# First block of an attention and MoE chain: U kept in SBUF from float32 products on 64x32 tiles, attention by head parity, added sums by DMA, a written issue order

## The chip, the cores and the metric

The kernel runs on one core of one Trainium2 chip. The metric is the device time of one execution in microseconds. Before, three runs took 1742.01, 1742.24 and 1744.55 us.

## What is computed

Slot attention over 8 batches, 8 heads, 576 tokens of width 64 and 32 slots, then two MLP blocks (512 to 2048 to 512) over all 4608 tokens. Weights come as float64.

```python
a   = softmax(phi, over tokens)                 # per slot
k_m = einsum('bhsm,bhsd->bhmd', a, k); v_m = einsum('bhsm,bhsd->bhmd', a, v)
attn = softmax(q @ k_m^T / 8, over slots)
x   = attn @ v_m                                # [4608, 512], heads side by side
x   = relu(x @ w_in)**2 @ w_out                 # first block
h   = x @ w_in2
out = (h - tanh(h)) @ w_out2                    # second block
```

## The kernel before, in words

Every product that needs float32 accuracy is split into a rounded part and a rest (fp32r), and three products are summed.

- **Attention, first half** (`att_a`, lines 169 to 260), for four heads of one batch: the softmax of phi over tokens, then `vkm` (line 216, 96x32 tiles, float32) and its transpose, which gives k_m and v_m.
- **U = v_m @ w_in** (lines 262 to 331). x is never formed; the first block multiplies attn by U, 256 rows (head, slot) by 2048 columns per batch. Batches 0 and 1 get U head group by head group (`u_first`). Batches 2, 3 and 4 to 7 are two groups: w_in's split lies in DRAM (`w_d`), `u_pair` computes a head for all batches of the group (lines 311, 312), copies it out, stores it to DRAM (`u_d`, line 315), and `u_load` (line 330) reads one batch's 512 columns back. U is held as float32.
- **Attention, second half** (`att_b`, lines 336 to 398), for half a batch: transpose q, scores, softmax over slots, transposes on VectorE, split into `at`.
- **First block** (`l1_step`, lines 446 to 503): units of 288 tokens, 16 units, 16 hidden tiles each, so 256 steps. A step casts 128 columns of U (450), subtracts (452), makes six products h (459), relu (463), the square (467 on ScalarE for s < 72, 469 on VectorE after), the split gh, gl (473, 475), and twelve products with w_out into four PSUM banks (483 to 485). The first four units take the hidden tiles in two halves; the sum of the first half goes to DRAM (503), comes back (512) and is added on VectorE (492).
- **Weights** (`conv`, lines 123 to 145): float64 words are made into float32 by one ScalarE and four VectorE instructions (133 to 143); `split` makes the fp32r pair on ScalarE and POOL (148, 150). The second block's weights are split in the first block, stored as pairs (`w2_d`) and loaded from POOL near its end (545, 551).
- **Second block** (lines 557 to 654): 144 steps of 12 products with w_in2 (595), the polynomial for h - tanh h (607 to 615), the split (624, 625), 12 products with w_out2 (639 to 641). `x2_load` splits x2 (576, 579).
- **Order.** The start, up to about step 36 of the first block, follows the string `ORDER`, one stage per word. From there tables of step numbers (`ATT_A`, `ATT_B`, `U_ALL`, `U_LOAD`, `W2_CONV`) say at which step a generator begins; each tick lets every active generator go on by one stage, and the framework's scheduler sets the order on the engines. Each engine then works its list in order; a DMA is issued in order by SyncE or POOL.

Of the kernel before, what the change touches and what calls it, by code (L numbers as in the profile page):

```python
# [41 lines left out]
ORDER = """
i0 i0 i0 i0 i1 c4 i0 c1 i1 c4 c4 c2 k0 i0 c1 i1 c2 i1 c13 b0 i0 c4 i0 c1 b0 b0 c0 i0 c2 c3 c1 i0 i0 c2 b0 b2 i0 c0 k1 c4 b0 c9 i1 b2 i1 i0 b2 b0 c0 i0 b2 c2 i1 b0 i0 b0 b1 c3 b2 b2 c3 i1 c9 c9 i1 c0 b0 b3 b1 b1 i1 b2 c1 i1 b0 b1 c7 b2 c5 c3 b1 i1 c9 b0 b5 i1 c0 i1 c9 u00 b2 c5 b5 b5 u00 b2 i1 b1 b5 b1 c3 c5 b0 c6 c5 b0 c6 b2 b3 b5 c7 b1 b1 b5 b0 c6 u01 u01 b1 b0 k2 i2 b3 b1 b3 s1 b3 c8 t2 i2 b2 b3 b1 c12 c6 t1 b3 s2 b1 c26 i2 b1 b1 s1 i2 s2 b3 c10 t3 c5 s0 b4 c12 i2 c11 s1 s0 i2 s0 s1 c6 c8 s0 s2 i2 c8 s1 c10 s0 i2 i2 c10 c8 i2 c8 c13 t0 s1 s2 s0 s1 c10 s2 b2 s3 b3 c12 b2 u02 s0 i2 u02 c11 c14 c11 c12 c10 s0 s3 b3 b2 b4 i2 i2 b3 s2 c11 c11 i2 i2 c7 c14 b4 s1 u03 b3 u10 c26 b4 b4 b3 u03 c13 b3 s2 c7 b3 c25 s3 c12 s2 b4 s4 s6 s5 s5 c25 s3 c7 c15 s3 s5 s5 s3 s4 b4 s6 c14 s4 s5 c13 s6 s8 s8 s3 s7 t11 c13 s4 s5 s6 s6 s7 s5 s4 c15 i3 c25 s3 s8 s4 s6 s10 k3 s4 c15 s8 s5 s7 s9 s8 s9 s4 c14 s7 s11 s9 c15 c30 s6 c14 s6 s7 s7 u10 c15 s9 s8 s10 s9 c26 s9 s7 i3 s10 s7 c17 s11 i3 s8 i3 s10 s11 s13 c26 s8 s10 s7 s14 s10 s7 i3 c30 s9 s14 c26 b4 s14 c25 s12 b4 c17 b7 s7 i3 s9 s12 c25 s13 s12 b7 s11 c17 i3 s14 s11 i3 b7 s12 i3 b4 s13 s15 s12 s12 i3 i3 s10 s11 u12 b7 b4 i3 b4 i3 i3 s14 u12 s12 s13 s11 s13 i3 c16 s10 s14 b5 s15 u11 c16 b5 b6 b5 b7 c17 b5 s15 b6 u11 s17 s14 b4 s11 c22 s13 b5 b6 b5 s19 s12 s15 s13 s14 s17 s15 c17 s16 b4 c30 s15 b6 s16 b6 b5 b4 b5 t10 b7 t26 t8 c16 b5 b6 s18 s13 s16 s15 s16 c28 b6 s17 b6 c30 s15 u13 c30 s16 c16 b6 s16 s19 s15 c16 s17 b6 s18 c29 b7 s17 s18 t9 s15 s16 b6 s19 s16 b7 s17 c22 u13 s18 b6 c20 b6 c19 s20 s19 s20 s21 b6 s17 s23 s19 s20 s23 s21 c22 s18 c19 b7 s18 s17 b6 s15 s20 s20 s22 s20 s18 s22 b7 s21 s18 s20 s29 c22 b7 s22 s20 s19 s19 b7 s19 s22 s29 s21 c19 s24 c20 b7 s23 b7 u04 s21 s21 c28 t25 s21 s25 s23 s22 s21 c18 b7 c20 s24 s23 c22 c20 s23 t16 s22 s29 c28 s22 c20 t17 c29 s29 s24 s25 s22 s30 s29 s24 s26 c28 c24 s23 s25 s24 s24 s25 s23 s24 u04 s27 s23 c28 c29 c29 c19 s25 s28 u14 c29 s27 c19 s25 s26 s26 s23 s28 c18 s26 s27 s24 s29 c27 s26 c18 s26 s31 s23 c27 c18 s27 s25 s30 s31 c21 s26 s28 c24 s27 c18 s25 s26 s28 t18 u05 s27 u05 s28 s33 s29 s28 s27 s32 s31 c27 s33 s30 s31 s30 s32 c23 s34 c21 s30 s29 s28 s32 s30 c24 s31 s35 s28 c23 s31 s31 t19 c21 s35 c23 c21 s30 s33 c21 u14 s33 s34 c27 s33 c24 c31 s32 c23 s27 s32 u15 s33 s30 c24 s33 c31 c27 c31 s32 s31 s34 s34 u06 c23 u07 u15 u06 s32 s31 u07 s35 s36 s34 s36 s32 s34 s34 s35 c31 t27 s35 c31 t24 s31
"""
# [3 lines left out]
ATT_A = (29, 33, 36, 39, 61, 65, 68, 71, 82, 76, 79, 86)  # L48
ATT_B = (47, 60, 76, 95, 107, 124, 146, 156, 176, 193, 205, 220)
U_ALL = (45, 46, 47, 48, 52, 52, 53, 54, 40, 56, 53, 54, 59, 55, 61, 62, 96, 95, 107, 108, 99, 100, 105, 101,  # L50
    110, 103, 120, 109, 113, 116, 125, 127)
U_LOAD = (58, 63, 63, 70, 88, 88, 78, 101, 123, 127, 129, 134, 143, 143, 150, 163, 181, 177, 177, 192, 193,
    200, 207, 222)
W2_CONV = (72, 68, 68, 76, 76, 83, 88, 88, 114, 115, 116, 123, 117, 128, 131, 130, 137, 139, 141, 149, 148,
    151, 160, 152, 166, 160, 179, 174, 185, 212, 207, 178)
# [7 lines left out]
def moe_chain_kernel(ctx: ExitStack, tc: tile.TileContext, q, k, v, phi, w1i, w1o, w2i, w2o, out):  # L63
    nc = tc.nc
    w1i, w1o, w2i, w2o = (w.bitcast(I32) for w in (w1i, w1o, w2i, w2o))
    out_v = out.rearrange("(b p c) e -> b c p e", b=B, c=NC)
# [42 lines left out]
    km_t = [a_km.tile([P, 4, 64], F32, name=f"km{i}") for i in range(5)]  # L109
    # v_m: for batches 0, 1 heads 0 to 3 of a group in 6 blocks of M columns: v0, v1, 0, 0, v2, v3; then [head, batch, M].  # L110
    vm = [a_v.tile([P, 32, M], F32R, name=n) for n in ("vh", "vl")]
    vh, vl = (t.rearrange("p (h b) m -> p h (b m)", h=H) for t in vm)
    v_done, v_read, s_done = set(), set(), set()
    for t in vm:
        nc.gpsimd.memset(t.bitcast(F32), 0.0)
    for t in km_t:
        nc.gpsimd.memset(t, 0.0)

# [1 line left out]
    raws = [p_raw, p_wob, p_u, p_u] + [p_raw, p_wob] * 12  # L120
    n_raw = [0]

    def conv(src, out):
        raw = slot(raws[n_raw[0]] if n_raw[0] < len(raws) else p_raw, [P, 512, 2], "raw", I32)
        n_raw_of = n_raw[0]
        n_raw[0] += 1
# [5 lines left out]
        f = slot(p_t, [P, 512], "wf")  # L132
# [19 lines left out]
    def half(o):  # L152
        return slice(64 * o, 64 * o + 64)
# [15 lines left out]
    def att_a(b, g, p_kv, ps, fine):  # L169
# [13 lines left out]
        if fine:  # L183
            yield
# [6 lines left out]
        if fine:  # L191
            yield
# [31 lines left out]
        if fine:  # L224
            yield
# [529 lines left out]
```

## Time and profile before

| What | Value |
|---|---|
| median of three runs | 1742.24 us |
| span of the profiled execution | 1736.6 us |
| TensorE busy | 1622.8 us (93%) |
| VectorE busy | 1331.5 us (77%) |
| ScalarE busy | 837.0 us (48%) |
| POOL busy | 721.6 us (42%) |
| moved by DMA | 185.27 MB |
| mean granted TensorE clock | 0.971 |

The page gives the profiled execution's own time as its span, from the first to the last instruction, 5.6 us under the median. Busy times are unions of overlapping instructions of one engine; shares are averages over stages with different limits, so the rows below are read by stretch.

### The profile page before, as it was taken

What the parts mean: (1) busy time and instruction counts of PE and PEld (TensorE: products, weight loads), DVE (VectorE), ACT (ScalarE), POOL (GpSimd) and SP (SyncE); (2) the same over time, 40 slices, a digit from 0 to 9 for tenths busy, and PEclk for the clock granted to TensorE, in tenths of its full rate; (3) what the DMA queues carried; (4) which work ended last, traced back from release to release, by engine and by line L of the source; (5) the groups of instructions that cost most, each with busy time, mean ns of one, the idle gap of its engine ahead of it and who ended that gap; (6) DMA issues with size and microseconds to landing.
All of it is one profiled execution on the core that took longest, in us unless ns stands there. A gap on an engine that the chain in (4) does not pass through costs nothing.

```text
span 1736.6 us, 27125 instructions
## 1 busy us (share of the span) xinstructions
PE 1622.8 (93%) x9488; PEld 1392.4 (80%) x9488; DVE 1331.5 (77%) x2016; ACT 837.0 (48%) x1875; POOL 721.6 (42%) x721
## 2 busy tenths in 40 slices
PE   5799997689998889999999999999999999999998
PEld 3588885578876788999998888888888888888887
DVE  7989642269635778785754898989898989898987
ACT  4677653245533555555554444444444444444343
POOL 4566532146533445554475342424242423232222
PEclk9899998789999999999999999999999999999999
DMA  9655664367845655341367010101010000000000
GB/s 256 200 172 191 192 183 146 103 183 224 251 141 186 209 173 182 113 161 55 104 222 238 1 38 12 31 19 31 19 28 22 26 24 25 25 7 25 1 25 25
DMA packets 114248, 185.27 MB, mean 107 GB/s; under 512 B 14272, under 2 KB 74688, under 8 KB 114112
## 3 DMA queue, kind: packets, MB, share of 16 engines
q1 hardware_dynamic: 104896, 149.99, 28.2%
q0 software_dynamic: 9216, 33.56, 6.1%
q8 instruction: 74, 1.21, 0.3%
q14 instruction: 62, 0.51, 0.1%
HBM read 124.52 MB, written 58.98 MB: 106 GB/s over the span
## 4 chain that ended last, share of the span: by engine, by line
PE 71%; DMA 13%; DVE 9%; issue 3%; POOL 2%; ACT 1%; SPq 0%; DVEq 0%; POOLq 0%; ACTq 0%
PE h L595 22%; DMA u_d<-ust 9%; PE o L641 8%; PE o L639 8%; PE o L640 8%; PE h L459 7%; PE acc L484 5%; PE acc L483 5%; PE acc L485 5%; DVE usp L452 1%; DVE wf L138 1%; DVE wf L143 1%; DVE wf L135 1%; DMA xs<-x_d 1%; DVE wf L137 1%
## 5 line engine op out<-in xcount | busy, mean ns | idle before, releaser
L625 POOL TENSOR_TENSOR gl<-pl,gh 128x512 fp32r<-128x512 f32 x144 | 206.1, 1431 | 519.2 <-ACT gh L624 519.2
L595 PE MATMUL h<-x2h,wi 128*128 128x512 f32 x1152 | 379.8, 391 | 0.0
L475 POOL TENSOR_TENSOR gl<-gg,gh 128x288 fp32r<-128x288 f32 x256 | 227.6, 891 | 316.5 <-ACT gh L473 267.2
L483 PE MATMUL acc<-gh,wo 128*128 128x288 f32 x1024 | 311.8, 305 | 18.9 <-DVE xs L492 16.6
L484 PE MATMUL acc<-gl,wo 128*128 128x288 f32 x1024 | 311.8, 304 | 5.5 <-POOL gl L475 5.4
L485 PE MATMUL acc<-gh,wo 128*128 128x288 f32 x1024 | 309.4, 302 | 0.0
L459 PE MATMUL h<-aT,usp 128*128 128x288 f32 x1536 | 272.7, 311 | 22.5 <-ACT r L463 9.6
L459 PEld LDWEIGHTS h<-aT,usp 128*128 128x128 f32 x1536 | 224.5, 195 | 43.7 <-issue 13.4
L595 PEld LDWEIGHTS h<-x2h,wi 128*128 128x128 f32 x1152 | 216.2, 188 | 46.4
L607 ACT ACTIVATE u<-h 128x512 f32<-128x512 f32 x144 | 86.2, 599 | 332.2 <-PE h L595 327.3
L639 PE MATMUL o<-wo,gh 128*128 128x512 f32 x576 | 225.4, 391 | 0.9 <-ACT gh L624 0.9
L641 PE MATMUL o<-wo,gl 128*128 128x512 f32 x576 | 224.9, 391 | 0.7 <-POOL gl L625 0.7
L640 PE MATMUL o<-wo,gh 128*128 128x512 f32 x576 | 224.3, 389 | 0.0
L595 PE MATMUL h<-x2l,wi 128*128 128x512 f32 x576 | 224.1, 389 | 0.0
L483 PEld LDWEIGHTS acc<-gh,wo 128*128 128x128 f32 x1024 | 200.5, 196 | 20.5 <-DVE xs L492 17.5
L484 PEld LDWEIGHTS acc<-gl,wo 128*128 128x128 f32 x1024 | 201.1, 196 | 8.5 <-POOL gl L475 8.2
L469 DVE TENSOR_TENSOR gg<-r 128x288 f32<-128x288 f32 x184 | 121.4, 660 | 112.2 <-ACT r L463 56.4
L485 PEld LDWEIGHTS acc<-gh,wo 128*128 128x128 f32 x1024 | 200.4, 196 | 0.0
L611 DVE SCALAR_TENSOR_TENSOR pl<-pl,u 128x512 f32<-128x512 f32 x144 | 184.0, 1278 | 4.5
L473 ACT CAST gh<-gg 128x288 fp32r<-128x288 f32 x256 | 110.0, 431 | 155.5 <-DVE gg L469 83.2
L452 DVE TENSOR_TENSOR usp<-u,usp 128x256 fp32r<-128x256 f32 x256 | 142.8, 561 | 41.4 <-ACT usp L450 41.1
L610 DVE SCALAR_TENSOR_TENSOR pl<-u 128x512 f32<-128x512 f32 x144 | 117.9, 819 | 43.0 <-ACT u L607 40.2
(100 smaller groups left out, 2643.7 us busy)
## 6 DMA issues: line engine op xcount, KB each, us to landing
raw<-in_moe_w_out SPq DMA_DIRECT2D x32, 512.0 KB
raw<-in_moe_w_in SPq DMA_DIRECT2D x32, 512.0 KB
ws<-w_d POOLq DMA_DIRECT2D x32, 512.0 KB, 6.8
w_d<-ws SPq DMA_DIRECT2D x32, 512.0 KB
u<-u_d SPq DMA_DIRECT2D x24, 512.0 KB
x_d<-xs SPq DMA_DIRECT2D x80, 144.0 KB
kv<-in_v SPq DMA_DIRECT2D x64, 144.0 KB
kv<-in_k SPq DMA_DIRECT2D x64, 144.0 KB
```

What stands on the lines that cost most here:

```text
L452: nc.vector.tensor_tensor(us[:, 1], src, us[:, 0].bitcast(F32), op=ALU.subtract)
L459: nc.tensor.matmul(t[:, :HT], us[:, w, g, :], x, start=(n == 0), stop=(n == 5))
L475: nc.gpsimd.tensor_tensor(gl, gg, gh.bitcast(F32), op=ALU.subtract)
L483: nc.tensor.matmul(o, wh[:, c], gh, start=(f == a), stop=False)
L484: nc.tensor.matmul(o, wh[:, c], gl, start=False, stop=False)
L485: nc.tensor.matmul(o, wl[:, c], gh, start=False, stop=(f == z - 1))
L595: nc.tensor.matmul(t, wi[f][:, w, c, :], x, start=(n == 0), stop=(n == 11))
L611: stt(pl, pl, A1, u, op0=ALU.add, op1=ALU.mult)
L625: nc.gpsimd.tensor_tensor(lo, pl, hi.bitcast(F32), op=ALU.subtract)
L639: nc.tensor.matmul(o, gh[:, c], wh, start=(f == 0), stop=False)
L640: nc.tensor.matmul(o, gh[:, c], wl, start=False, stop=False)
L641: nc.tensor.matmul(o, gl[:, c], wh, start=False, stop=(f == FT - 1))
```

## The change

- **U.** w_in stays float32 (`w1`, no split). `u_make` multiplies v_m of one head (64x32, at rows 0 to 63 or 64 to 127 of the array by the head's parity and at 32 columns by its pair) by 512 columns, eight products into two banks (line 246), and writes cast and rest of 512 columns straight into an SBUF tile that the steps read (250, 251). Four such tiles exist, so a tile is made once both units of the batch before have read theirs. `u_d`, `w_d`, the stores and loads of U and the per-step cast are gone. w_in is kept in DRAM as float32 (135) and reloaded for each batch from 2 on, 1 MB for 512 columns (140).
- **Attention.** `att_b` takes four heads of one parity over the whole batch: scores as eight 64x32 products into two banks (293), softmax on 128x576. `att_a` adds tokens in two halves.
- **First block.** The square is always on ScalarE (386). The half sums of the first four units are added in DRAM by an accumulating DMA that POOL issues (417). `tmp` has six buffers, not eight.
- **Second block's weights** are stored as float32 (431) and split after the reload (438, 446 with `split`): w_out2 and seven tiles of w_in2 in the last 22 steps of the first block, nine tiles of w_in2 in the second block's first steps.
- **Order.** The whole first block is issued as written: each iteration s emits the first products of step s + 3, ScalarE's part of s + 2, the second products of s, and then one stage of each background generator whose resources (`free`: PSUM banks b, buffers) are there.

```diff
+    def u_make(b, fc):
+        while not {("a", b, g) for g in range(2)} | {("w", fc, pr) for pr in range(4)} <= done:
             yield
+        yield "b b u"
+        w = w1[0 if b < 2 else b, fc]
+        t = [psum(ps_b, f"u{o}") for o in range(2)]
+        for i in range(4):
+            for o in range(2):
+                nc.tensor.matmul(t[o][32 * i:32 * i + 32], vt[b][half(o), i], w[half(o), i])
+        yield "-"
+        u = slot(p_u, [P, 2, 2, 512], f"u{b}_{fc}", F32R)
         for o in range(2):
+            nc.scalar.copy(u[:, 0, o], t[o])
+            nc.vector.tensor_tensor(u[:, 1, o], t[o], u[:, 0, o].bitcast(F32), op=ALU.subtract)
+        give("b", "b")
...
+    def tick(new=()):
+        for gen in new:
+            active.append(gen)
+            wants[gen] = ""
+        for gen in sorted(active, key=lambda gen: wants[gen] != "-"):
+            need = collections.Counter(wants[gen].strip("-").split())
+            if any(free[r] < n for r, n in need.items()):
+                continue
+            free.subtract(need)
...
+    def l1_out(u, a):
+        outs = [slot(p_t, [P, HT], "xs") for _ in range(ET)]
+        for e in range(ET):
+            (nc.vector.tensor_copy if e % 2 else nc.scalar.copy)(outs[e], acc[u][e][:, :HT])
+        yield
+        for e in range(ET):
+            if a:
+                nc.gpsimd.dma_start(x2_d[u][e], outs[e], accum_op=ALU.add)
+            else:
+                nc.sync.dma_start(x2_d[u][e], outs[e])
...
+    for s in range(T0, N1):
...
+        l1_mm1(s + 3)
+        l1_act(s + 2)
+        if s >= 0:
+            l1_mm2(s)
...
+        new, plan[s] = plan.get(s, ()), ()
+        tick(new)
```

What this moves, at three places. First TensorE, around one group of U products of a later batch. Before (acc are the sums of the unit, ws the split w_in, vh and vl the split v_m):

```order
L485 MATMUL acc_3_4077<-gh,wo 128x288
L311 MATMUL u_4203<-ws,vh 64x512
L312 MATMUL u_4203<-ws,vl 64x512
L311 MATMUL u_4209<-ws,vh 64x512
L312 MATMUL u_4209<-ws,vl 64x512
L459 MATMUL h<-aT,usp 128x288 x6
```

And with the change:

```order
L404 MATMUL acc_3_5309<-gh,wo 128x288
L246 MATMUL u_5644<-w_1_5356,vt_4538 32x512
L246 MATMUL u_5645<-w_1_5356,vt_4538 32x512
L246 MATMUL u_5644<-w_1_5356,vt_4538 32x512
L246 MATMUL u_5645<-w_1_5356,vt_4538 32x512
L246 MATMUL u_5644<-w_1_5356,vt_4538 32x512
L246 MATMUL u_5645<-w_1_5356,vt_4538 32x512
L246 MATMUL u_5644<-w_1_5356,vt_4538 32x512
L246 MATMUL u_5645<-w_1_5356,vt_4538 32x512
L372 MATMUL h<-aT_3945,u_3_4951 128x288 x6
```

Two heads for a group of batches, each as a sum of two products, become eight heads for one batch in single products that alternate between two banks.

Second VectorE in the first block's later steps. Before:

```order
L469 TENSOR_TENSOR gg<-r 128x288
L452 TENSOR_TENSOR usp<-u_0_7806,usp 128x256
L469 TENSOR_TENSOR gg<-r 128x288
L452 TENSOR_TENSOR usp<-u_1_7808,usp 128x256
L469 TENSOR_TENSOR gg<-r 128x288
L452 TENSOR_TENSOR usp<-u_1_7808,usp 128x256
```

And with the change, where nothing of a single step stands on VectorE any more:

```order
L251 TENSOR_TENSOR u_3_4951<-u_4910,u_3_4951 128x512
L251 TENSOR_TENSOR u_3_4951<-u_4911,u_3_4951 128x512
L302 STREAM_TRANSPOSE sm<-sc_4956 128x288
L302 STREAM_TRANSPOSE sm<-sc_4957 128x288
L306 TENSOR_REDUCE mx_4997<-sm 128x18
L285 COPY qt<-qT_5002 128x288
L285 COPY qt<-qT_5070 128x288
```

Third POOL, at the end of the first block. Before (w_d are split weights in DRAM):

```order
L475 TENSOR_TENSOR gl<-gg,gh 128x288
L551 DMA wo<-w_d_12_217 128x1024
L551 DMA wo<-w_d_13_218 128x1024
L551 DMA wo<-w_d_14_219 128x1024
L551 DMA wo<-w_d_15_220 128x1024
L579 TENSOR_TENSOR x2l<-x2f,x2h 128x512 x2
L625 TENSOR_TENSOR gl<-pl,gh 128x512 x14
```

And with the change (w2f is a reloaded weight, x2f a reloaded x2):

```order
L390 TENSOR_TENSOR gl<-gg,gh 128x288
L467 TENSOR_TENSOR x_10504<-x2f,x_10503 128x512
L149 TENSOR_TENSOR wo<-w2f,wo 128x512
L467 TENSOR_TENSOR x_10504<-x2f,x_10503 128x512
L149 TENSOR_TENSOR wo<-w2f,wo 128x512 x5
L149 TENSOR_TENSOR wi_10791<-w2f,wi_10791 128x512
L149 TENSOR_TENSOR wi_10846<-w2f,wi_10846 128x512
L149 TENSOR_TENSOR wi_10893<-w2f,wi_10893 128x512
L513 TENSOR_TENSOR gl<-pl,gh 128x512
```

Four issues of loads and two subtractions between the last gl of the first block and the first of the second become eleven subtractions.

## Rows read from the trace of the kernel before

**Rows 1.** Busy time by stretch; columns PE, PEld, DVE, ACT, POOL, clock, DMA share.

```profile
0.00:61.90 61.90, 37.43 (x245) 24.84 (x246) 51.39 (x83) 32.24 (x68) 29.05 (x41) 0.94 0.92 259
...
61.90:240.00 178.10, 160.41 (x1255) 145.80 (x1254) 141.65 (x223) 120.32 (x312) 105.74 (x108) 0.97 0.61 182
...
240.00:400.00 160.00, 127.15 (x790) 102.25 (x790) 65.81 (x131) 61.15 (x158) 48.23 (x65) 0.82 0.46 145
...
640.00:940.00 300.00, 292.31 (x2163) 281.89 (x2162) 211.80 (x392) 156.63 (x418) 172.31 (x201) 0.99 0.46 151
```

**Rows 2.** First product with w_out (line 483), and first of the second block.

```profile
L483 PE MATMUL acc<-gh,wo x1024: 290/294/609, 62.1 to 940.0; 128*128 128x288 f32 x171
...
940.39 0.40 PE L595 MATMUL h<-x2h,wi 128*128 128x512 f32 x1
```

**Rows 3.** TensorE in order of time, two steps late in the first block.

```profile
849.23 0.96 PE L459 MATMUL h<-aT,usp 128*128 128x288 f32 x6
...
851.63 0.96 PE L459 MATMUL h<-aT,usp 128*128 128x288 f32 x6
```

**Rows 4.** Busy time by stretch of line 485 alone (PE and PEld).

```profile
61.90:240.00 178.10, 57.08 (x190) 36.85 (x191) 0.97 0.61 182
...
640.00:940.00 300.00, 135.97 (x459) 86.98 (x458) 0.99 0.46 151
```

**Rows 5.** The page, chain that ended last, by line.

```profile
PE h L595 22%; DMA u_d<-ust 9%; PE o L641 8%; PE o L639 8%; PE o L640 8%; PE h L459 7%; PE acc L484 5%; PE acc L483 5%; PE acc L485 5%; DVE usp L452 1%; DVE wf L138 1%; DVE wf L143 1%; DVE wf L135 1%; DMA xs<-x_d 1%; DVE wf L137 1%
```

**Rows 6.** Instructions by line: busy us, mean ns of one, idle before and releasers.

```profile
L452 DVE TENSOR_TENSOR usp<-u,usp 128x256 fp32r<-128x256 f32 x256 | 142.8, 561 | 41.4 <-ACT usp L450 41.1
...
L450 ACT CAST usp<-u 128x256 fp32r<-128x256 f32 x256 | 101.6, 399 | 12.8 <-PE h L459 6.6 <-DMA u<-u_d 6.2
...
L469 DVE TENSOR_TENSOR gg<-r 128x288 f32<-128x288 f32 x184 | 121.4, 660 | 112.2 <-ACT r L463 56.4
...
L613 DVE TENSOR_TENSOR th<-h,th 128x512 f32<-128x512 f32 x144 | 98.4, 683 | 0.0
...
L138 DVE SCALAR_TENSOR_TENSOR wf<-raw,wf 128x512 int32<-128x512 int32 x64 | 60.8, 951 | 1.4
...
L475 POOL TENSOR_TENSOR gl<-gg,gh 128x288 fp32r<-128x288 f32 x256 | 227.6, 891 | 316.5 <-ACT gh L473 267.2
...
L150 POOL TENSOR_TENSOR ws<-wf,ws 128x512 fp32r<-128x512 f32 x48 | 67.0, 1396 | 49.0 <-ACT ws L148 39.1 <-PE acc L484 5.4 <-DVE mx L369 3.1
```

**Rows 7.** Float32 products: two lines' durations (min/median/max), then TensorE in time.

```profile
L216 PE MATMUL vkm<-kv,e x768: 269/273/423, 12.6 to 457.1; 96*32 96x128 f32 x192
...
L360 PE MATMUL sc<-qt,km x128: 406/457/742, 25.1 to 865.9; 128*64 128x288 f32 x128
...
406.90 0.44 PE L350 MATMUL qT<-ident,qr 96*128 96x96 f32 x3
407.12 0.64 PE L459 MATMUL h<-aT,usp 128*128 128x288 f32 x3
...
433.20 0.30 PE L485 MATMUL acc<-gh,wo 128*128 128x288 f32 x1
433.43 1.79 PE L216 MATMUL vkm<-kv,e 96*32 96x128 f32 x48
...
865.55 0.71 PE L360 MATMUL sc<-qt,km 128*64 128x288 f32 x4
```

**Rows 8.** VectorE in order of time, four instructions of the start.

```profile
8.45 0.41 DVE L135 TENSOR_SCALAR wf<-wf 128x512 f32<-128x512 f32 x1
...
9.35 0.69 DVE L138 SCALAR_TENSOR_TENSOR wf<-raw,wf 128x512 int32<-128x512 int32 x1
...
10.68 0.94 DVE L194 TENSOR_TENSOR e<-phi,mb 96x768 f32<-96x768 f32 x1
...
59.50 4.20 DVE L138 SCALAR_TENSOR_TENSOR wf<-raw,wf 128x512 int32<-128x512 int32 x1
```

**Rows 9.** DMA issues: count, KB each, median us from issue to landing.

```profile
ws<-w_d POOLq DMA_DIRECT2D x32, 512.0 KB, 6.8
```

More of the change, by code (lines that the diff above doesn't have):

```diff
@@ L44 @@
[L44 to L55, printed above, removed]
@@ L107, in psum, with give, half, conv @@
         return p.tile([P, 512], F32, tag=p.name, name=name)
[L109 to L126, printed above, removed]
+    free = collections.Counter(b=2, f=3, kv=1, ph=1, q=1, e=1, vn=1, vt=2, kt=2, qt=1, sm=1, at=2, w1=2, u=FC)
+    def give(*rs):
+        free.update(rs)
+    def half(o):
+        return slice(64 * o, 64 * o + 64)
+    def conv(src, out, p=None):
+        raw = slot(p or p_raw, [P, 512, 2], "raw", I32)
         dst = raw.rearrange("p n t -> p (n t)")
@@ L138, in conv, with w1_conv, w1_load @@
         stt(fi, raw[:, :, 1], -0x40000000, fi, op0=ALU.bitwise_and, op1=ALU.bitwise_or)
-        low = stt
-        if n_raw_of in POOL_LOW:
+        stt(fi, raw[:, :, 0], 29, fi, op0=ALU.logical_shift_right, op1=ALU.bitwise_or)
+        yield
+        return f
+    w1_d = {fc: p_d.tile([P, 4, 512], F32, name=f"w1_d{fc}") for fc in range(FC)}
+    w1 = {}
+    def w1_conv(fc, pr, p=None):
+        if pr == 0:
+            yield "w1"
+            w1[0, fc] = slot(p_w, [P, 4, 512], f"w1_{fc}")
+        while (0, fc) not in w1:
             yield
-            low = nc.gpsimd.scalar_tensor_tensor
-        low(fi, raw[:, :, 0], 29, fi, op0=ALU.logical_shift_right, op1=ALU.bitwise_or)
+        t = w1[0, fc][:, pr]
+        yield from conv(w1i[pr * P:(pr + 1) * P, fc * 1024:(fc + 1) * 1024], t, p)
+        done.add(("w", fc, pr))
         yield
-        yield from out(f)
+        nc.sync.dma_start(w1_d[fc][:, pr], t)
+    def w1_load(b, fc):
+        yield "w1"
+        w1[b, fc] = slot(p_w, [P, 4, 512], f"w1_{fc}")
+        nc.sync.dma_start(w1[b, fc], w1_d[fc])
+        yield
+    wo = {}
     def split(f, hi, lo):
@@ L232, in att_a @@
                              AF.Copy, scale=den)
-        yield
-        t = psum(ps3, "vkmT")
+        give("b")
+        yield "b" if g else "b vt kt"
+        t = psum(ps_b, "vkmT")
         for i in range(2):
             nc.tensor.transpose(t[:, i * P:(i + 1) * P], n[:, i].rearrange("p t d -> p (t d)"), ident)
-        if fine:
-            yield
-        if b not in km:
-            assert b < 5 or all((b - 5, x, y) in s_done for x in range(2) for y in range(2)), b
-            km[b] = km_t[b % 5]
@@ L284, in u_wload @@
[L284 to L297 removed]
+        give("vn")
@@ new lines, in moe_chain_kernel, with att_b @@
+    at = {}
+    done = set()
+    sc_done = collections.Counter()
+    def att_b(b, o, p_q):
+        if p_q is a_q:
+            yield "q"
+        qs = slot(p_q, [SP, 4, NC, D], f"q{b}_{o}")
+        nc.sync.dma_start(qs, q[b, o::2].rearrange("h (p c) d -> p h c d", c=NC))
+        yield
+        yield "qt"
+        qt = slot(a_qt, [P, 4, HT], "qt")
+        for i in (0, 2):
+            yield "b b"
+            t = [psum(ps_b, f"qT{i}") for _ in range(2)]
+            for n in range(2):
+                for c in range(3):
+                    nc.tensor.transpose(t[n][:, c * SP:(c + 1) * SP],
+                                        qs[:, i + n, 2 * c:2 * c + 2, :].rearrange("p c d -> p (c d)"), ident[:SP, :SP])
+            if i and p_q is a_q:
+                give("q")
+            yield "-"
+            nc.scalar.copy(qt[:, i], t[0][:, :HT])
+            nc.vector.tensor_copy(qt[:, i + 1], t[1][:, :HT])
+            give("b", "b")
+        while not {("a", b, g) for g in range(2)} <= done:
+            yield
+        yield "b b sm"
+        t = [psum(ps_b, f"sc{r}") for r in range(2)]
+        for i in range(4):
+            for r in range(2):
+                nc.tensor.matmul(t[r][32 * i:32 * i + 32, :HT], kt[b][half(r), 2 * i + o], qt[half(r), i, :])
+        give("qt")
+        sc_done[b] += 1
+        if sc_done[b] == 2:
+            give("kt")
+        yield "-"
+        s = slot(a_sm, [P, 18, M], "sm")
+        s2 = s.rearrange("p t m -> p (t m)")
+        for r in range(2):
+            nc.vector.transpose(s2[:, r * HT:(r + 1) * HT], t[r][:, :HT])
+        give("b", "b")
+        mx = p_s.tile([P, 18], F32, tag="mx9", name="mx9")
+        sm = p_s.tile([P, 18], F32, tag="sm9", name="sm9")
+        nc.vector.reduce_max(mx, s, axis=AX.X)
+        yield
+        nc.gpsimd.tensor_tensor(s, s, mx.unsqueeze(2).to_broadcast([P, 18, M]), op=ALU.subtract)
@@ L318, in u_all @@
[L318 to L319 removed]
+        nc.vector.reduce_sum(sm, s, axis=AX.X)
+        nc.vector.tensor_scalar(sm, sm, 1e-9, None, op0=ALU.add)
+        nc.vector.reciprocal(sm, sm)
         yield
+        nc.gpsimd.tensor_tensor(s, s, sm.unsqueeze(2).to_broadcast([P, 18, M]), op=ALU.mult)
         yield
[L322 to L331 removed]
@@ L400, in both @@
-    def both(g0, g1):
-        next(g0)
-        next(g1)
-        yield
-        next(g0)
-        yield
-        for _ in g0:
-            next(g1)
-            yield
-        for _ in g1:
-            yield
-    active = []
-    def tick(new=()):
-        active.extend(new)
-        for gen in list(active):
+        a = slot(a_sm, [P, 2 * HT], "aT")
+        nc.vector.transpose(a, s2)
+        yield "" if b in at else "at"
+        if b not in at:
+            at[b] = slot(p_at, [P, 2, 2, 2 * HT], f"aT{b}", F32R)
@@ L734 @@
+    order.__exit__(None, None, None)
+    plan = {k - N1 - 3: g for k, g in plan.items() if k >= N1}
+    for s in range(-3, N2):
+        tick(plan.pop(s, ()))
+        l2_gsplit(s + 2)
+        l2_mm1(s + 3)
+        l2_act(s + 3)
+        l2_mm2(s)
+        j, f = divmod(s, FT)
+        if 1 <= j < NB - 1 and f == 0:
+            for c in (0, 2):
+                at_step(s + 1 + 3 * (c // 2), x2_load(j + 1, c, p_x2f))
 _INS = ['q', 'k', 'v', 'phi', 'moe_w_in', 'moe_w_out', 'moe2_w_in', 'moe2_w_out']
```

591 lines of the change are left out of this document (207 added, 384 removed).

## The prediction, made before the changed kernel ran

> **What bounds the kernel now.** I read four views, in this order: busy time by stretch, TensorE's instructions in order of time, the groups of instructions by line, and the chain of waits. The first shows where the time lies. Until 61.9 us no product with w_out runs; 256 steps of the first block follow until 940.4 us, where the second block's first product starts [rows 1, 2]. The chain of waits runs through that block's products (lines 595 and 639 to 641 hold 46% of it, 799 us) [rows 5], and the change leaves them as they are, so from 940.4 to the end of the span, 1736.6 − 940.4 = 796.2 us, I take over whole. The question is the first block. Undisturbed, a step repeats every 851.63 − 849.23 = 2.40 us [rows 3], so 256 steps need 613 us; they take 940.4 − 61.9 = 878.5. Counting products of line 485, four to a step, shows where [rows 4]: 190 records up to 240 us are 47.5 steps at 3.7 us, 459 after 640 us are 115 steps at 2.6, and the 94 steps between take 400 us, 4.3 each. The reader is to see three different limits in them. Up to 240 us VectorE is 142 of 178 us busy; from 240 to 400 every engine idles and the granted clock is 0.82 on average; after 640 TensorE is busy 292 of 300 us [rows 1]. The chain of waits names the second: stores and loads of U through DRAM (u_d) are 9% of the whole chain, 156 us [rows 5].
>
> **The change, part by part**, against the span.
>
> *The second U trip goes.* For batches 2 to 7 before, U is computed by group, stored to DRAM and read back; now it goes from PSUM straight to SBUF. The u_d wait on the chain has no successor of its kind. What is late next is TensorE's own queue, so I rebuild the first block from its work instead of subtracting 156.
>
> *Steps.* They keep their 18 products of 288 columns: 256 × 2.40 = 613 us. The split of U moves from each step (561 ns on VectorE, 399 on ScalarE, 256 times) [rows 6] to 64 pieces of 512 columns. The square moves wholly to ScalarE, where it stands in the place of the U cast. VectorE loses 143 us of U split and 121 of squares (184 × 660 ns) [rows 6] and gains 64 × 683 = 44 us (line 613's row prices a 512-column subtraction with a PSUM operand) [rows 6]. After 640 us VectorE works 211.8 / 115 = 1.84 us a step and ScalarE 1.36 [rows 1, 4]; the one loses 1.2 of it, the other stays, so both hide under a step's 2.40.
>
> *U's products.* 256 products of 64x32 tiles, 512 columns, plain float32, replace the fp32r ones. No row has this form. The column price: two recorded passes per float32 product, at least 269 ns each at 128 columns and 406 at 288 [rows 7], so (406 − 269) / 160 = 0.86 ns a column and 0.44 us a pass at 512. Eight products one after another take 16 × 0.44 = 7.0 us; all eight at once 0.88 plus the 0.2 of a fill. The nearest row is the 96x32 group: 48 passes of 128 columns in 1.79 us [rows 7] against 48 × 0.11 = 5.3 alone, a 2.9-fold overlap of four tiles. Eight tiles at that yield make 5.9-fold, 1.2 us a group. Bounds: 1.1, and 2.4 if only the column tiles overlap, since no row shows two row halves at work together. I take 1.2, nearest that row: 32 × 1.2 = 38 us, bounds 35 and 77.
>
> *Other background on TensorE after the start.* Per batch: two vkm groups, two of 1.79 [rows 7], 3.6; eight triples of q transposes and eight small products of the first half, each like the triple that held the queue for 407.12 − 406.90 = 0.22 us [rows 7], 3.5, and 0.4 for the array's switches around them; scores 1.4 (two groups at 0.71 [rows 7]); four U groups, 4.8. That is 13.7 us. Six batches and the rest of batches 0 and 1 (six U groups and a little): 82 + 10 = 92 us.
>
> Around these groups the array is switched between whole and tiled use. The row shows 433.43 − 433.20 = 0.23 us from the last whole product to the first tiled one against 2.40 / 18 = 0.13 between whole products [rows 3, 7]: a tenth, inside my 1.2. The Trainium skill (TensorEngine Tiling (Array Packing), Key Properties) says instead that changing the tiling mode drains the engine, and gives no time; if a drain were worth a whole 0.30 us product, 64 switches would make about 13 us more.
>
> *The start.* The order puts VectorE at its limit until the first step: up to the transpose that ends the first batch's attn it has 114 instructions, 64 of them in 16 conversions. In the first 61.9 us before, 83 such instructions were 51.39 us of work, 0.62 each, and 83% of the time [rows 1]; 114 are 71 us, and 85 at that density. A conversion is 10.68 − 8.45 = 2.23 us undisturbed [rows 8], and up to 3.1 if all its parts suffer as line 138 does on average (951 ns for 0.69) [rows 6, 8]: 7 us either way for 16. The last cast, subtraction and the first step's chain add some 6. SyncE adds to it: four stores of converted w_in wait for VectorE ahead of the next nine loads. I add 3 and take 94 us for the first product with w_out (before 61.9 [rows 2]), bounds 86 and 112. The change starts later and then runs faster.
>
> *Waits that I expect to stay.* Steps 0 to 24: twelve conversions, up to 37 us of VectorE, beside attention in some 65 us, and two buffers for raw weights; 25 us, between 5 and 50. The four sums added by DMA: POOL issues them, and ScalarE needs their tiles again within two steps, with six temporaries in place of eight. The nearest price is POOL's w_d load, 6.8 us to landing [rows 9], against roughly 4 of slack: 3 each, 12, between 0 and 32. The other unit ends and background groups: 10, between 0 and 30. In the last 12 steps POOL has a gl of 0.89 and 1 to 1.5 splits of w_out2, w_in2 or x2 at 1.4 [rows 6] against 2.40 a step: 9 us late. Sum 56.
>
> *The seam.* Before, POOL only issued loads there. Now eleven splits stand on POOL between the last gl and the second block's first, 11 × 1.4 = 15 us, while TensorE can fill in four sets of products with w_in2: 796.2 us / 144 steps / 2 = 2.76 each, 11 us. VectorE suffers too: at 59.50 one operation took 4.20 us in place of 0.69 [rows 8], with POOL at work without a gap beside it. I take 14 us, between 4 and 25.
>
> **Sum.** 94 + 613 + 92 + 56 = 855 for the second block's start, before 940.4; with 14 and 796.2 the span is 1665. The runs' median, 1742.24, lies 5.6 above the span of the profiled execution, which I keep: **1671 us**.
>
> **Rivals.**
> *A. The 64x32 tiles do not overlap* (slower). Place: the 32 U groups. One after another they cost 32 × 7.0 = 224 in place of 38: 1671 + 186 = 1857 us. It decides from 3.4 us a group on, where the gain of 71 is gone. Against it: column tiles start within one short row of each other in the vkm group. For it: no row with two row halves. 4%.
> *B. TensorE waits in line for PSUM banks.* Every background group takes banks that VectorE or ScalarE must empty first, and a conversion of 2.2 to 3.1 us may stand ahead. 18 groups a batch in seven batches are 126; 0.57 us each beyond my 10 eats the gain. 0.35 would give 1715, 0.9 some 1775. Against: after 640 us, with second halves of attention under way, only 7.7 of 300 us idle [rows 1]; and the new order puts the emptying a step ahead of the next use. 10%, about a third of it slower.
> *C. No waits to speak of.* Start at 86, waits of 10, seam of 5: 1671 − 8 − 46 − 9 = 1608; half of that, 1640, is likelier. 8%.
> *D. U was hidden anyway, and the start decides.* If the chain's 156 us are only a label for a VectorE limit that stays, steps 0 to 64 keep their 3.7 to 4 us and the start's loss of 32 remains: about 1735, no difference. Against: VectorE is only 66 of 160 us busy from 240 to 400 [rows 1]. 3%.
>
> **How the numbers follow.** The forecast's own case has 75%; its bounds added the way independent errors add (start 15, U 25, waits 30, seam 8) make some 40 us each way. The range, 1630 to 1718, takes in half of C and the nearer part of B. Faster: 75 + 8 + 6 of B and a little of D, 0.90; same, within 0.2% (3.5 us, what a measurement of this kernel tells from nothing): 0.03; slower 0.07.
>
> **What would show it.** Right: first product with w_out near 94 us; U groups (line 246) of eight products in about 1.2 us; the second block's start near 855; no u_d in the chain; steps after 64 at some 2.8 us with background; TensorE waiting for POOL for several us at the seam. Wrong: U groups over 2.4 us; TensorE idle by lines 279, 293 or 206 waiting for VectorE copies; ScalarE's relu waiting for the added sums by more than 5 us; a start beyond 112.

## The result, and the profile after

The changed kernel takes 1765.55 us (median of four runs, 1761.74 to 1766.28) against 1742.12 for the kernel before: a ratio of 1.0133, 95% interval 1.0117 to 1.015. It is slower by 1.3%; 1671 us, faster by 4%, was forecast. The profiled execution spans 1760.0 us. These are single lines' instructions on TensorE in the changed kernel (count: shortest/median/longest ns, first and last start): products with w_out, U's products, products with w_out2, and the longest wait ahead of these (us, times).

```profile
L402 PE MATMUL acc<-gh,wo x1024: 288/294/583, 110.3 to 853.4; 128*128 128x288 f32 x171
...
L246 PE MATMUL u<-w,vt x512: 589/613/1060, 58.7 to 764.8; 64*32 64x512 f32 x171
...
L527 PE MATMUL o<-wo,gh x576: 387/389/796, 869.9 to 1753.5; 128*128 128x512 f32 x192
...
  ACT osb L534: 59.7, 8
```

The products with w_out2 in the kernel before:

```profile
L639 PE MATMUL o<-wo,gh x576: 389/389/499, 952.4 to 1730.1; 128*128 128x512 f32 x192
```

They cut the span into four pieces. The first block's last product with w_out starts at 853.4 us, before at 940.0 [rows 2]; 855 was forecast for the block's end. All that was lost lies behind it: from the first product with w_out2 to the end of the span 1736.6 − 952.4 = 784.2 us before, 1760.0 − 869.9 = 890.1 now. That is 143.75 steps between first and last such product in 883.6 us, 6.15 a step; before 777.7, 5.41 a step. The lines of the second block's 24 products a step are the same.

Busy time by stretch (columns as in [rows 1]), the changed kernel, and below it the kernel before in the stretch that [rows 1] leaves out:

```profile
0.00:110.30 110.30, 47.48 (x373) 28.93 (x374) 69.92 (x123) 32.16 (x63) 29.39 (x35) 1.00 0.66 199
...
240.00:400.00 160.00, 158.56 (x1389) 146.92 (x1388) 75.28 (x124) 98.83 (x232) 81.72 (x91) 1.00 0.61 168
...
1000.00:1300.00 300.00, 274.88 (x1163) 222.36 (x1162) 228.97 (x295) 116.49 (x212) 82.80 (x61) 0.95 0.08 22
```

```profile
1000.00:1300.00 300.00, 300.00 (x1316) 246.61 (x1315) 269.50 (x336) 135.64 (x240) 102.60 (x70) 1.00 0.09 25
```

The hole of 240 to 400 us is closed (TensorE 127 busy before, 159 now [rows 1]). From 1000 to 1300 every engine does less than before: none has become the bound. So something waits in a circle. Who waited for whom in that stretch (us in total, times, longest), changed kernel and kernel before:

```profile
POOL gl L513 <- ACT gh L512: 212.3, 47, 5.7
ACT gh L512 <- DVE pl L503: 171.5, 45, 4.0
DVE pl L498 <- ACT u L495: 63.1, 46, 1.8
```

```profile
POOL gl L625 <- ACT gh L624: 185.9, 50, 5.3
ACT u L607 <- PE h L595: 121.2, 52, 3.3
ACT gh L624 <- DVE pl L615: 35.9, 27, 3.5
DVE pl L610 <- ACT u L607: 12.9, 31, 1.3
```

Before, ScalarE waits above all for TensorE. Now it waits for VectorE, and VectorE for ScalarE. One step on ScalarE and then on VectorE, changed kernel:

```profile
1011.17 0.62 ACT L512 CAST gh<-pl 128x512 fp32r<-128x512 f32 x1 [3.96 <-DVE pl L503]
1011.70 0.59 ACT L495 ACTIVATE u<-h 128x512 f32<-128x512 f32 x1
1012.19 0.59 ACT L496 ACTIVATE th<-h 128x512 f32<-128x512 f32 x1
1012.66 0.73 ACT L497 ACTIVATE m<-u,neg_umax 128x512 f32<-128x512 f32 x1
1017.32 0.62 ACT L512 CAST gh<-pl 128x512 fp32r<-128x512 f32 x1 [3.93 <-DVE pl L503]
```

```profile
1012.39 1.31 DVE L498 SCALAR_TENSOR_TENSOR pl<-u 128x512 f32<-128x512 f32 x1 [1.33 <-ACT u L495]
...
1016.45 0.75 DVE L503 COPY_PREDICATED pl<-m,th 128x512 f32<-128x512 int32 x1
```

And ScalarE in the kernel before:

```profile
1013.63 0.60 ACT L607 ACTIVATE u<-h 128x512 f32<-128x512 f32 x1 [3.27 <-PE h L595]
1014.13 0.61 ACT L624 CAST gh<-pl 128x512 fp32r<-128x512 f32 x1
1014.63 0.60 ACT L608 ACTIVATE th<-h 128x512 f32<-128x512 f32 x1
```

Before, the square u of step s + 3 stands ahead of the cast gh of step s + 2. Now it stands behind it. The cast waits for VectorE's last operation of step s + 2, so VectorE, which needs u to begin step s + 3, stands still meanwhile. The circle: cast to square 0.53 us, square to VectorE's first operation 0.69, VectorE 4.81 (1012.39 to 1017.20), back to the cast 0.12; sum 6.15, the step that was measured. TensorE needs 5.5 (24 products, 0.23 us apart); it runs ahead and pays at eight of the nine output tiles, where its first product waits 7.5 us for the copies of line 534 that stand in ScalarE's queue (59.7 us, above).

The text of the second block has the cast first in both kernels; the scheduler, which orders this block, moved the square ahead of it before and does not now. Two differences of this block are missing from the list of changes ahead of the prediction: the tile pl comes from the pool `wf` (three buffers) and no longer from `tmp`, and the sums of an output tile have four names and no longer five.

### The profile page after: what moved, and what is told of

Read it like the earlier page. It is cut to its first block, busy times and chain, and to the rows that moved or that the text cites. A ratio compares the mean times of both kernels' runs of the same rounds, so it can differ in the third digit from the quotient of the medians.

```text
span 1760.0 us, 26494 instructions
## 1 busy us (share of the span) xinstructions
PE 1582.2 (90%) x9904; PEld 1351.0 (77%) x9904; DVE 1055.1 (60%) x1500; ACT 832.6 (47%) x1743; POOL 644.1 (37%) x602
## 4 chain that ended last, share of the span: by engine, by line
DVE 16%; issue 14%; PE 11%; ACT 5%; POOL 4%; DMA 1%; ACTq 0%; DVEq 0%; POOLq 0%; SPq 0%
PE h L483 5%; DVE pl L498 4%; POOL gl L513 3%; DVE pl L503 3%; DVE pl L499 3%; DVE pl L502 2%; DVE u L500 2%; ACT gh L512 2%; DVE th L501 2%; PE o L527 2%; PE o L529 2%; PE o L528 2%; ACT u L495 2%; POOL x L467 1%; ACT m L497 0%
## 5 line engine op out<-in xcount | busy, mean ns | idle before, releaser
L483 PE MATMUL h<-x,wi 128*128 128x512 f32 x1728 | 425.7, 395 | 10.7 <-DVE th L501 4.1
L483 PEld LDWEIGHTS h<-x,wi 128*128 128x128 f32 x1728 | 326.3, 189 | 86.0 <-DVE th L501 4.5
L512 ACT CAST gh<-pl 128x512 fp32r<-128x512 f32 x144 | 89.3, 620 | 533.2 <-DVE pl L503 505.3
L527 PE MATMUL o<-wo,gh 128*128 128x512 f32 x576 | 235.3, 408 | 65.1 <-ACT osb L534 59.7
L498 DVE SCALAR_TENSOR_TENSOR pl<-u 128x512 f32<-128x512 f32 x144 | 178.4, 1239 | 184.0 <-ACT u L495 179.2
L372 PE MATMUL h<-aT,u 128*128 128x288 f32 x1536 | 258.5, 304 | 10.5 <-ACT r L384 7.6
L372 PEld LDWEIGHTS h<-aT,u 128*128 128x128 f32 x1536 | 217.3, 190 | 44.9 <-ACT gh L389 14.5
L528 PE MATMUL o<-wo,gh 128*128 128x512 f32 x576 | 232.4, 404 | 0.0
L527 PEld LDWEIGHTS o<-wo,gh 128*128 128x128 f32 x576 | 112.4, 195 | 97.4 <-ACT osb L534 63.1
L529 PEld LDWEIGHTS o<-wo,gl 128*128 128x128 f32 x576 | 112.8, 196 | 43.0 <-POOL gl L513 18.1
L528 PEld LDWEIGHTS o<-wo,gh 128*128 128x128 f32 x576 | 113.2, 196 | 23.9
L386 ACT ACTIVATE gg<-r 128x288 f32<-128x288 f32 x256 | 113.9, 445 | 31.3 <-POOL gl L390 8.6
```

The costliest lines, as they stand in the source:

```text
L372: nc.tensor.matmul(t[:, :HT], uu[:, w, o, c], at[u // 2][:, x, o, u % 2 * HT:u % 2 * HT + HT], start=(n == 0), stop=(n == 5))
L483: nc.tensor.matmul(t, wi[f][:, w, c, :], x, start=(n == 0), stop=(n == 11))
L498: stt(pl, u, A2, u, op0=ALU.add, op1=ALU.mult)
L512: nc.scalar.copy(hi, pl)
L527: nc.tensor.matmul(o, gh[:, c], wh, start=(f == 0), stop=False)
L528: nc.tensor.matmul(o, gh[:, c], wl, start=False, stop=False)
```

## The experiments

**Theory.** ScalarE's order closes a loop with VectorE, and the loop sets the step. **Rival 1.** Four tiles for the second block's sums (before: five names rotating over four banks) make TensorE wait for the copies. **Rival 2.** The seam: the scheduler mixes the second block's first products into the first block's tail. "By hand" means below that the second block, from its step 12 on, is issued in the order of its text. In the edits shown, "..." stands for further lines.

**m_same**, by hand, nothing else:

```diff
+    order = tc.manual_schedule()
     for s in range(-3, N2):
+        if s == 12:
+            order.__enter__()
...
```

> The changed kernel with the second block issued by hand in the order in which its text stands, so on ScalarE: cast of step s+2 (it waits for VectorE's last operation of that step), then square, tanh and relu of step s+3. Nothing else differs, and the scheduler's mixing of the block's first products into the first block's tail goes. Theory (a loop between ScalarE and VectorE: the square that VectorE waits for stands behind the cast that waits for VectorE): the order is the same in every step, so a step stays at about 6.15 us and the time at 1765, within 10. Rival 1 (four banks for the sums in place of a rotation over five tiles): the same, 1765. Rival 2 (the scheduler's mixing at the seam set TensorE back for good): about 1680.

1795.75 us (1.0307, 1.0292 to 1.0323; in brackets, here and below, the ratio to the kernel before and its 95% interval). The seam is not the cause: of the 26 products with w_in2 that stood ahead of the last product with w_out, 7 are left there, and the time did not fall. It is 30 us over the changed kernel, 20 beyond the expected range. Most steps take 6.16 us in both (median spacing of VectorE's first operation), but the casts and splits of x are now spread over four steps of an output tile, which take 7.1 each: 41 steps over 6.4 us, in the changed kernel, whose scheduler bundles them, 17.

**m_sqfirst**, m_same with the square (`l2_sq`, taken out of `l2_act`) ahead of the cast:

```diff
...
-        l2_gsplit(s + 2)
         l2_mm1(s + 3)
+        l2_sq(s + 3)
+        l2_gsplit(s + 2)
         l2_act(s + 3)
```

> As m_same, but the square of step s+3 stands ahead of the cast of step s+2 on ScalarE, as in the kernel before. Theory: VectorE can start step s+3 while the cast waits, TensorE becomes the bound of the second block again at 24 products x 0.23 = 5.5 us a step, 144 x 0.64 = 92 to 106 us less: 1660 to 1675. Rival 1 (banks): TensorE goes on waiting some 7.5 us for the copies of line 534's kind at each of eight output tiles, 1745 or more. Rival 2 (the seam): no difference from m_same.

1661.27 us (0.9532, 0.9518 to 0.9546), 134 less than m_same. Waits from 1000 to 1300 us, and the products with w_out2:

```profile
POOL gl L520 <- ACT gh L519: 202.5, 55, 4.9
ACT u L493 <- PE h L483: 168.3, 55, 3.3
DVE pl L505 <- ACT u L493: 17.5, 48, 1.0
```

```profile
L534 PE MATMUL o<-wo,gh x576: 387/389/526, 867.7 to 1654.3; 128*128 128x512 f32 x192
```

ScalarE waits for TensorE again, a step is (1654.3 − 867.7) / 143.75 = 5.47 us, and with the same four tiles TensorE's wait for the copies is gone (1.1 us in all). The wait for the copies was a result of the loop, not its cause. Nor is it that POOL slows VectorE less here. VectorE's first two operations of a step, m_sqfirst and below it m_same:

```profile
L505 DVE SCALAR_TENSOR_TENSOR pl<-u 128x512 f32<-128x512 f32 x144 | 107.2, 744 | 47.4 <-ACT u L493 47.4
L506 DVE SCALAR_TENSOR_TENSOR pl<-pl,u 128x512 f32<-128x512 f32 x144 | 205.2, 1425 | 4.9
```

```profile
L498 DVE SCALAR_TENSOR_TENSOR pl<-u 128x512 f32<-128x512 f32 x144 | 189.0, 1313 | 188.4 <-ACT u L495 188.4
L499 DVE SCALAR_TENSOR_TENSOR pl<-pl,u 128x512 f32<-128x512 f32 x144 | 136.7, 949 | 4.9
```

Together they take 312 us here and 326 there, while the time differs by 134: the slow operation has moved from the first place to the second, and what is gone is most of VectorE's wait for the square (188 us there, 47 here).

**e2_pl_tmp**, the changed kernel with its scheduler: does pl's pool turn the order?

```diff
-        pl = slot(p_f, [P, 512], "pl")
+        pl = slot(p_t, [P, 512], "pl")
```

> The changed kernel, scheduler and all, with one word other: the tile pl of the second block comes from the pool of temporaries again (six buffers, now for four tiles a step) and not from the pool wf. In the listed order this alone puts the square ahead of the cast again in 14 of 16 steps. Theory: most of the loss goes, 1665 to 1690; the two steps with the cast first, beside the loads of x, may cost 1 us each. Rival 1 (banks): 1745 or more. Rival 2 (seam): 1765, or more, for six buffers hold fewer steps.

1683.76 us (0.9657, 0.9641 to 0.9674), 5.59 a step: as the theory has it.

**m_before_castfirst**, the kernel before by hand, cast first:

```diff
+        order = tc.manual_schedule()
         for s in range(-3, N2):
+            if s == 12:
+                order.__enter__()
             l2_gsplit(s + 2)
...
```

> The kernel BEFORE, with its second block issued by hand in the order of its text: the cast of step s+2 ahead of the square of step s+3 in every step. Five tiles for the sums, eight temporaries and the whole first block stay. Theory: the loss of the changed kernel appears here, 144 steps x 0.6 to 0.75 us: 1742 + 85 to 106 = 1827 to 1848. Rival 1 (banks): no change, 1742, since the five tiles stay. Rival 2 (seam): no change, 1742.

1873.12 us (1.0749, 1.0733 to 1.0765). The loss appears in the old kernel with five tiles, 130 us and not 85 to 106: its median step is 6.16 us too, and 36 steps, those with x2's splits among them, take over 6.4.

**b_pl_pool**, the kernel before with the scheduler and one word other:

```diff
-        pl = slot(p_t, [P, 512], "pl")
+        pl = slot(p_us, [P, 512], "pl")
```

> The kernel BEFORE with one word other and the scheduler left to work: the second block's tile pl comes from the pool of three that x2f uses (usp), not from the pool of temporaries. In the listed order ScalarE then stands as in the changed kernel: cast of step s+2, square, tanh, relu of step s+3, in nearly all steps. Theory (pl's move to another pool, a side edit, is what turned the scheduler's order, and the order is the loss): 6.15 us a step and more beside x's splits, 1840 to 1875, near the 1873 of the hand-ordered run. If pl's pool had no part in it: 1742, within 10.

1854.72 us (1.0632, 1.0612 to 1.0651). ScalarE's rows show the changed kernel's order:

```profile
1009.76 0.62 ACT L624 CAST gh<-pl 128x512 fp32r<-128x512 f32 x1 [3.96 <-DVE pl L615]
1010.28 0.59 ACT L607 ACTIVATE u<-h 128x512 f32<-128x512 f32 x1
```

Its median step is 6.16 us as well. So in either kernel the pool from which one tile comes decides the order. Why the scheduler turns with it is open.

**m_castlater**, m_same in which the cast stays first but takes an older step:

```diff
-        l2_gsplit(s + 2)
+        l2_gsplit(s + 1)
         l2_mm1(s + 3)
```

> m_same with one number changed: the cast, still ahead of the square on ScalarE, is now that of step s+1, whose last VectorE operation is a whole step old, in place of step s+2. If it is the WAIT of the cast that costs (the loop ScalarE to VectorE and back), the loss goes although the cast stays first: 1661 to 1675, as with the square first. If it were the position of the square as such, or the four banks, or POOL beside VectorE's first operation, it stays at 1750 to 1796. The splits come a step later, so TensorE may wait for POOL once in a while: up to 10 us.

1660.58 us (0.9532, 0.9506 to 0.9557). The wait of the cast costs, not its place. POOL's subtraction moves with the cast, and VectorE's first operation takes 0.70 us on average, so this run alone would not tell the wait from POOL's slowing; m_sqfirst does.

**m_same_psum**, m_same with one operand other: what a step of the loop consists of.

```diff
-        stt(pl, u, A2, u, op0=ALU.add, op1=ALU.mult)
+        stt(pl, u, A2, h, op0=ALU.add, op1=ALU.mult)
```

> m_same (1795.75; cast first, 6.15 us a step) with one operand other: VectorE's first operation of a step takes h from PSUM as its second factor in place of u from SBUF, so the polynomial's first factor is changed; every wait and the order stay. In m_same that operation takes 1.31 us while POOL's gl runs beside it, 0.69 undisturbed. If the loop of waits alone makes the loss: no change, 1790 to 1796. If the order costs by putting gl beside that operation in every step: the loop shrinks by 0.62 to 5.53 a step, which TensorE's 5.5 almost covers, and the time falls by 60 to 90, to 1705 to 1735, the steps with splits of x staying slower.

1765.29 us (1.0136, 1.011 to 1.0161): 30 us less than m_same, between the two expectations. VectorE's first operation fell to 0.69 us, but it now begins behind the tanh, which reads h as well (VectorE in order of time):

```profile
1014.62 0.69 DVE L498 SCALAR_TENSOR_TENSOR pl<-u,h 128x512 f32<-128x512 f32 x1 [1.81 <-ACT th L496]
1015.34 1.37 DVE L499 SCALAR_TENSOR_TENSOR pl<-pl,u 128x512 f32<-128x512 f32 x1
```

The loop lost 0.62 and gained 0.48: 6.01 a step, and 6.7 in place of 7.1 in some 38 steps beside x's splits. 105 × 0.15 + 38 × 0.4 = 31 us; 30 were measured. Both changes of the loop came through in full. A loop without POOL's slowing and with nothing added, 5.53 us, is shown by no run.

**The forecast's own terms**, each edit made on top of m_sqfirst (1661.27):

**m_utwice** issues each U group's eight products twice:

```diff
-        for i in range(4):
-            for o in range(2):
-                nc.tensor.matmul(t[o][32 * i:32 * i + 32], vt[b][half(o), i], w[half(o), i])
+        for _ in range(2):
+            for i in range(4):
+                for o in range(2):
+                    nc.tensor.matmul(t[o][32 * i:32 * i + 32], vt[b][half(o), i], w[half(o), i])
```

> m_sqfirst (1661.3) with the eight 64x32 products of every U group issued twice, the second time over the first's result. This prices the term of U's products: the forecast took 1.2 us a group, 38 in all, the trace of the changed kernel shows about 1.1. If the tiles overlap and TensorE's queue is the limit of the first block, 32 x 0.9 to 1.1 = 29 to 35 us are added, 1690 to 1697, less a few us at the start, where TensorE idles. If U is hidden in waits of TensorE: no more than 5 us. If eight products one after another cost 7 us (rival A): +220.

1680.41 us (0.9648, 0.9617 to 0.9679), 19 more. Sixteen products take 1.95 us in the trace, eight 1.09: 32 × 0.86 = 27.5 us, so some 8 did not reach the time; TensorE's idle time in the first block fell from 32.1 us (m_sqfirst) to 27.2, which accounts for 5 of them. U lies on the path, but less than whole; the expected 29 to 35 was too much.

**m_noclamp** (first edit) and **m_uone** (second), on the start:

```diff
-        nc.vector.tensor_scalar(f, f, W_HI, W_LO, op0=ALU.min, op1=ALU.max)
+        if p is not p_wo:
+            nc.vector.tensor_scalar(f, f, W_HI, W_LO, op0=ALU.min, op1=ALU.max)
```

```diff
-    at_step(T0 + 23, u_make(0, 1))
+    at_step(T0 + 32, u_make(0, 1))
```

> m_sqfirst without the clamp (one VectorE operation of 0.43 us out of four) in the 20 conversions whose raw weights lie in the buffers of wo, 16 of them ahead of the first step; the clamp is left out. Forecast's view (VectorE is at its limit until the first step): the first product with w_out comes 16 x 0.43 = 7 us earlier, at 104 to 105 in place of 111.7, and the time falls by as much. Rival (a chain of single handovers between the engines, in the hand-written order, sets the start; VectorE is busy only 70 of 111 us): the start moves by under 2 us and the time by under 3.

> m_sqfirst with batch 0's second U group nine steps later in the hand-written order (it is first needed in step 4): in the trace it stands on TensorE, with VectorE's conversions before it, between the first half's attention and the scores of the second half, from 77 to 87 us. If the start is a chain of handovers, the first product with w_out comes 3 to 8 us earlier, 104 to 109 in place of 111.7, and the time falls by that: 1653 to 1658. If VectorE is the limit there, nothing moves by over 2 us, for its work is the same.

m_noclamp: 1655.89 us (0.9508, 0.9482 to 0.9533), first product with w_out at 108.3. m_uone: 1660.86 us (0.9536, 0.9506 to 0.9565), first product at 114.1, later if anything. Kernels with the same start lie between 110.3 and 113.8. Leaving out 7 us of VectorE work (62.7 us of it ahead of the first product, 70.0 in m_sqfirst) so moved it by 3.4 us against m_sqfirst and 2 beyond that spread, between the two views; the U group gave nothing.

**m_storelate** (first edit), **m_lateconv** (second) and **m_both**, also on the start:

```diff
         done.add(("w", fc, pr))
-        yield
+        for _ in range(12 if fc < 2 else 1):
+            yield
         nc.sync.dma_start(w1_d[fc][:, pr], t)
```

```diff
     for i in range(12):
-        at_step(T0 + 5 + 1.4 * i, w1_conv(1, i - 4, p_wo) if 4 <= i < 8 else wo_conv(i if i < 4 else i - 4, p_wo))
+        at_step(T0 + 5 + 1.4 * i + (0 if i < 4 else 10 if i < 8 else 8), wo_conv(i, p_wo) if i < 4 else w1_conv(1, i - 4, p_wo) if i < 8 else wo_conv(i - 4, p_wo))
-    at_step(T0 + 23, u_make(0, 1))
+    at_step(T0 + 32, u_make(0, 1))
```

> m_sqfirst (1661.3) with the stores of the converted w_in of the first two column blocks twelve steps later in the hand-written order. In the trace SyncE issues only these four stores between 8.7 and 22.1 us, each waiting for a VectorE conversion, and the second half's loads and three of w_out stand behind them; VectorE then idles for 4 us. If SyncE's order is what made the start late, the first product with w_out comes 4 to 10 us earlier than 111.7. If not (the second half's phi waits for its only buffer until 22.1 anyway): under 2 us.

> m_sqfirst with eight of the sixteen conversions ahead of the first step (four of w_in's second column block, four of w_out) eight to ten steps later, and batch 0's second U group with them. VectorE's work ahead of the first step stays nearly the same, but 4 to 8 conversions of 2.23 us no longer stand ahead of the first scores' transposes on VectorE (in the trace they run from 46 to 57 us, with the scores' operand kt behind them at 52.1). If the start is the hand-written order's chain: 6 to 12 us earlier, 100 to 106. If VectorE's amount of work sets it: no change, within 2.

> Both of these edits. If the two waits are separate, their gains add: the first product with w_out at 95 to 102 and a time of 1645 to 1652; if one stands behind the other, no better than the better of the two.

m_storelate: 1656.15 us (0.9507, 0.9481 to 0.9533), first product at 108.7. m_lateconv: 1665.22 (0.9556, 0.9532 to 0.9581), 114.1. m_both: 1660.63 (0.9534, 0.9512 to 0.9557), 112.5. m_storelate's first product is 3 us earlier, between its two expectations; m_lateconv's is 2.4 us later, which neither of its own had; both edits together are no better than the first. SyncE's rows in m_storelate show why the first edit gave little; with the stores out of the way SyncE stands before the load of phi instead, whose one buffer VectorE reads until 22.6 us (in m_sqfirst the load was issued at 22.1, no later):

```profile
8.69 0.98 SPq L107 DMA_DIRECT2D raw<-in_moe_w_out  x1
22.64 0.34 SPq L167 DMA_DIRECT2D phi<-in_phi  x1
```

The 0.3% between m_storelate and m_sqfirst lies within the intervals; that both are 4.7% and more faster than the kernel before does not. The best versions that leave nothing out are m_sqfirst, m_castlater and m_storelate, at 1656 to 1661 us.

## Why the prediction was wrong

The step that failed is the first one: "the change leaves them as they are, so from 940.4 to the end of the span, 1736.6 − 940.4 = 796.2 us, I take over whole". The second block's lines are nearly untouched, but its order is not written, it is made by the scheduler, and one moved tile turned it: a step of 5.41 us became one of 6.15, and the 784 us of the forecast's sum became 890. No rival had it: A, B and D sought a loss in the first block or ahead of it, and C was a gain. The order of ScalarE's queue in the changed kernel's second block would have shown it ahead of time; the orders shown ahead of the prediction are those of TensorE, VectorE and POOL, in the first block and at its end.

The other terms, against the profiled execution:

| Term | Forecast | Measured |
|---|---|---|
| first product with w_out | 94 (86 to 112) | 110.3 |
| first block from there: steps, U, background, waits | 761 | 743.1 |
| of it U's products | 38 (35 to 77) | 33 (30 groups of 1.1) |
| of it other background | 54 | 45 |
| of it steps and waits | 669 | 655 |
| block's end | 855 | 853.7 |
| seam, over before | 14 (4 to 25) | 4 |
| rest | 784 | 890 |

The three shares are sums of the spacing between starts on TensorE by line; the missing 10 are products of the second block that the scheduler put among the last steps. With the order turned back, m_sqfirst's span of 1660.8 us is 4 from the forecast's 1665. That is luck in part: its start came 18 us later than forecast and its second block took 9 us more (793 from the first product with w_out2, not 784), while the first block took 16 less (744.6) and the seam 15 less. Two sums of the forecast are off by little: 256 × 2.40 is 614, not 613, and 0.9 us for each of rival B's groups gives 1784, not 1775.

- **Start.** 94 was worked out from VectorE at its limit. It did the 71 us of work that were counted (69.9), in 110.3 us instead of 85: 63% and not 83%. Taking 7 us of its work out gave 3, so its work alone is not the limit; moving single stores, conversions and a U group moved the start by 3 us at most, either way. What chain sets the start is open.
- **U.** Eight products of 64x32 take 1.09 us, 1.2 was forecast from the 2.9-fold overlap of four tiles. Rival A is refuted, and the two row halves do overlap: with column tiles alone 2.4 was forecast. The price that the prediction set on the Trainium skill's rule (TensorEngine Tiling (Array Packing), Key Properties: a change of mode drains the engine), 13 us, is not to be seen: the first U product starts 0.21 us after the last whole product, at 501.05 and 501.26 us, where whole products follow each other at 0.13.
- **Waits.** The added sums were costed at 12 us; ScalarE waits 5.3 us for their DMA in the whole block (lines 384 and 386), and TensorE 7.6 for the relu. All waits kept were put at 56; TensorE is idle for 26.8 of the block's 743.1 us. Rival B (waiting in line for PSUM banks) did not come: from 240 to 400 us TensorE is idle 1.4 of 160 us.
- **Seam.** From the last product with w_out to the first with w_out2 12.4 us before, 16.5 now, and 11.4 in m_sqfirst. The 4 of the table leave out the 26 products with w_in2, 9 us, that already stand in the first block. TensorE is idle for 6.0 us at the seam now, and for none in m_sqfirst, which has the same splits to make on POOL: they hardly cost there.
- **Rival D** is refuted: the first 42 steps take 3.1 us each (168 products of line 402, four to a step, in the 129.7 us up to 240), the next 57 take 2.8 (228 products in 160 us), where it had 3.7 to 4 up to step 64.

## What to carry to other kernels

Where a scheduler orders a stage, equal source lines are no equal order: one tile's pool turned it here, so compare each engine's order in every stage that the sum takes over whole. When all engines idle more in a stage and none is full, add up the circle of waits from one repetition of the timeline; if its sum is the step, look in the queues for the one instruction that waits with work behind it that its own releaser needs. Then move that work ahead, or let the waiting instruction take an older step.

## What the runs showed of the hardware

VectorE's first operation of a step (u plus a constant, times u, both from SBUF) has a median of 1.32 us in the changed kernel and 0.69 before; in the changed kernel POOL's gl (1.29 us) runs beside it in most steps. With one operand from PSUM it takes 0.69 with POOL at work beside it, while the next operation, both of whose operands lie in SBUF, takes 1.37 (rows of m_same_psum above; POOL's subtractions there start at 1013.61 and 1014.87 us and take 1.3 each). The Trainium skill (GPSIMD Engine Reference, Specifications) says that the two engines contend when a VectorE instruction has two SBUF inputs; these measurements agree. Which operation pays goes by the order: in m_sqfirst it is the second (rows above).

The granted clock was 0.95 on average from 1000 to 1300 us in the changed kernel. At one output tile there TensorE stands still for 7.7 us, until 1071.2; the clock was 1.00 (2.4 GHz) from 980 to 1063 us, 0.50 (1.2 GHz) from 1066.5 to 1076.5 and 1.00 again from 1080 to 1160. In the kernel before and in m_sqfirst, where TensorE is busy for all 300 us, it was 1.00.
